# Attention backward on Trainium2: all of dS turned by the DMA crossbar in fifteen of sixteen head pairs, with a fourth dS buffer and dQ half a group later

## The chip, the core and the metric

The kernel runs on one core of one Trainium2 chip. Its engines are TensorE (PE, with its weight loads PEld), VectorE (DVE), ScalarE (ACT), GpSimd (POOL) and SyncE (SP); each works through its own instructions in order, and they meet through semaphores. SP does no arithmetic: it issues DMAs. The metric is the device time of one execution in microseconds (us). Before the change it was 2538.72 us, the median of 3 runs (2536.06 to 2540.79).

## The reference

The reference is a transformer block with adaptive layer norm, and its whole backward pass: attention with 32 heads of width 16 over 2048 tokens, a squared-ReLU MLP, and the gradients of ten inputs. The output and all gradients are returned. What matters here is attention:

```python
def _A_ref(x, wqkv, wo):
    B, S, D = x.shape            # 1, 2048, 512
    H = 32
    Dh = D // H                  # 16
    qkv = (x @ wqkv).reshape(B, S, 3, H, Dh).transpose(2, 0, 3, 1, 4)
    q, k, v = qkv[0], qkv[1], qkv[2]
    scores = jnp.einsum('bhqd,bhkd->bhqk', q, k) * Dh ** (-0.5)
    p = _softmax(scores, axis=-1)
    o = jnp.einsum('bhqk,bhkd->bhqd', p, v)
    return o.transpose(0, 2, 1, 3).reshape(B, S, D) @ wo
...
_out, _vjp = jax.vjp(_f, A_x, A_wqkv, A_wo, B_w1, B_b1, B_w2, B_b2, c, w_mod)
_grads = _vjp(grad_out)
```

For each head the backward pass computes P again from Q and K, then dP = dO V^T, dS = P (dP - rowsum), dK = dS^T Q, dV = P^T dO and dQ = dS K. The first two of the gradients sum over queries and the last over keys, so dS is wanted with queries on the partitions and, turned, with keys on the partitions.

## The kernel before, in words

The stages follow each other: forward attention, MLP forward and backward, attention backward (`attn_bwd`, L1429), and an end stage (`phase6`) with the gradients of Wqkv, of the modulation and of x. The change is in attention backward.

**Loops.** The heads are taken two at a time: 8 quads `g` of four heads, each with two pairs `jp`, so 16 pairs. In each pair `c` runs over 4 chunks of 512 keys, and `ib0` over 4 groups of G = 4 query blocks of 128. A pair thus has 16 groups, the stage 256. In a group, `i` runs over 4 units; a unit is one query block by one key chunk for both heads (`a` = 0, 1).

**One unit.** For each head PE makes the scores `st` (L1584, 64 rows of K, 512 columns) and, for the unit before (`last`), the product `dp` (L1509); ACT takes exp of `st` into `pu` (L1587); DVE multiplies `dp` by `pu` into dS (L1513). `st` and `dp` have three PSUM buffers each. In every second unit PE adds two older units to the dK and dV sums (`kv_two`, `kv`, L1455, 8 matmuls); in the others it adds up to dQ (`dq`, L1478). After the last query block of a chunk ACT copies the dK and dV sums out (`kvT`, L1458). At a pair's end these are turned on PE and copied by ACT (`turn`, L1468 and L1472, in two halves), and dQ is scaled by DVE (L1483), turned on PE (`turn_q`, L1491) and copied by ACT.

**Odd groups.** `off(c, ib)` is true in every second group. There one of the eight products of a group (unit 0, second head) goes to another place: ACT copies `dp` to SBUF (L1521) and POOL multiplies (L1522). DVE does 15 products in two groups, POOL one.

**Turning dS.** A group's dS is one buffer `ds` of 128 x 4096 bf16, 32 blocks of 128 x 128; there are three (`self.dsp`, pool `p5ds`). `turn_ds` (L1535) is called in the group's unit 2. In odd groups it only takes a destination `dsT` (four buffers). In even groups it turns the first four blocks on PE into an `st` buffer (L1543), and ACT copies them to `dsT` (L1544). When the last product of the group is made, `dS` (L1524) has SP issue one transposing DMA (L1530) for the rest: 32 blocks in odd groups, 28 in even ones.

**dQ.** When that DMA is issued, eight entries of four matmuls each go to `pendq`. In units 0 and 2 of each group, while more than 4G = 16 entries wait, four entries are taken out (eight, if more than 6G = 24 wait). A new destination or buffer waits for those who used it last; this is done by semaphores that the framework puts in.

**Order.** PE, SP and POOL follow the order of the program text; the framework orders DVE and ACT. POOL issues the loads of the next pair's operands piece by piece (`pieces`, L1573), each behind a one-element copy of dS (`tick`, L1572).

**`keep`.** A tile of 128 x 8192 bf16. Its first 2048 columns hold K of every second quad. In the last pair (g, jp) = (7, 1) the pieces that POOL issues fill all of it with the normalised x for the end stage; until then the other columns are not used.

**The end.** After the loop the remaining entries of dQ are drained in three lots, between matmuls of the end stage (`dw_mm`).

Of the kernel before, what the change touches and what calls it, by code (L numbers as in the profile page):

```python
# [9 lines left out]
BF16 = mybir.dt.bfloat16  # L10
# [9 lines left out]
P = 128  # L20
# [85 lines left out]
class K:  # L106
# [1230 lines left out]
    def phase5(self):  # L1337
        S, D, NQ, ST, DT = self.S, self.D, self.NQ, self.ST, self.DT
        nc, io = self.nc, self.io
        opa = self.open_pool("p56a", bufs=1)  # L1340
        self.pup = self.open_pool("p5pu", bufs=6)
        self.dq_t = opa.tile([P, ST, D], BF16, name="dq_t")
        self.dk_t = opa.tile([P, ST, D], BF16, name="dk_t")
        self.dv_t = opa.tile([P, ST, D], BF16, name="dv_t")
        self.opa = opa
        self.junk6 = opa.tile([P, D], F32, name="junk6")
        nc.gpsimd.memset(self.dsa_part[:], 0.0)
        assert ST * self.H == D
        self.cs = [self.csq[:], self.rl[:].rearrange("p s h -> p (s h)"), self.mod_25[:, 1, :]]
        self.parts = [self.dq_t, self.dk_t, self.dv_t]  # L1350
        self.stp = self.open_pool("p5st", bufs=3, space=PSUM)
        self.dpp = self.open_pool("p5dp", bufs=3, space=PSUM)
        self.kvp = self.open_pool("p5kv", bufs=1)
        self.dsp = self.open_pool("p5ds", bufs=3)
        self.dtp = self.open_pool("p5dt", bufs=4)
        self.accp = self.open_pool("p5acc", bufs=1, space=PSUM)
        self.attn_bwd()
# [71 lines left out]
    def attn_bwd(self):  # L1429
# [7 lines left out]
        tc, nc = self.tc, self.nc  # L1437
        S, D, H, NQ, ST, SC = self.S, self.D, self.H, self.NQ, self.ST, self.SC
        G = 4
# [7 lines left out]
        pend, pendq, turnq = [], [], []  # L1447
# [12 lines left out]
        def turn(g, jp, kvT, s0):  # L1460

            if kvT is None:
                return turn_q(g, jp)
            h0 = 4 * g + 2 * jp
            n = ST // 2
            tp = stp.tile([P, n, P], BF16, name="st")
            for st in range(n):
                nc.tensor.transpose(tp[:, st, :], kvT[:, (s0 + st) * P:(s0 + st + 1) * P], self.ident[:])  # L1468
            v = tp[:].rearrange("p s (t a e) -> p t s a e", t=2, a=2)
            for t, dst in enumerate((self.dk_t, self.dv_t)):  # L1470
                d = dst[:, s0:s0 + n, h0 * DH:(h0 + 2) * DH].rearrange("p s (a d) -> p s a d", a=2)
                nc.scalar.copy(d, v[:, t, :, :, 0:DH])  # L1472
# [31 lines left out]
        def dP(u, a):  # L1504

            (T, g, jp, c, ib, kvT, pu, dsg, i, grp) = u
            rd = slice(64 - 64 * jp, 128 - 64 * jp)
            dp = dpp.tile([P, 512], F32, name="dp")
            nc.tensor.matmul(dp[:], lhsT=T["dOT"][rd, ib * P:(ib + 1) * P],  # L1509
                             rhs=masked["VT"][a][rd, 512 * c:512 * (c + 1)], start=True, stop=True)  # L1510
            if a == 1 and i == 0 and off(c, ib):
                return dp
            nc.vector.tensor_tensor(dsg[:, i, a], dp[:], pu[:, a, :], ALU.mult)  # L1513

        def off(c, ib):
            return (c * SC + ib // G) % 2 == 1

        def dP_pool(u, dp):
            (T, g, jp, c, ib, kvT, pu, dsg, i, grp) = u
            f = (self.junk6, self.csq)[(c * SC + ib // G) // 2 % 2]  # L1520
            nc.scalar.copy(f[:], dp[:])  # L1521
            nc.gpsimd.tensor_tensor(dsg[:, i, 1], f[:], pu[:, 1, :], ALU.mult)  # L1522

        def dS(u):  # L1524

            (T, g, jp, c, ib, kvT, pu, dsg, i, grp) = u
            pend.append((T, g, jp, c, ib, kvT, pu, dsg[:, i]))
            if i == G - 1:
                dsT, n = grp
                nc.sync.dma_start_transpose(dsT[:, n:, :], dsg[:].rearrange("p i a k -> p (i a k)")[:, n * P:])  # L1530
                for a in range(2):
                    for sub in range(4):
                        pendq.append((T, g, jp, c, ib - G + 1, a, sub, dsT))

        def turn_ds(dsg, grp, skip):  # L1535

            dsT = dtp.tile([P, 8 * G, P], BF16, name="dsT")
            grp.extend((dsT, 0 if skip else 4))
            if skip:
                return  # L1540
            tp = stp.tile([P, 4, P], BF16, name="st")
            for b in range(4):
                nc.tensor.transpose(tp[:, b, :], dsg[:, 0, 0, b * P:(b + 1) * P], self.ident[:])  # L1543
            nc.scalar.copy(dsT[:, 0:4, :], tp[:])  # L1544

        tick = self.tick
        T = self.T0
        last = None
        for g in range(NQ):
            for jp in range(2):  # L1550
                if jp == 0:
                    if g + 1 < NQ:
                        Tn, later = self.load_group(g + 1)
                    else:
                        Tn, later = None, self.wq_pieces(1) + self.load_wmt()
                    cut = len(later) // 2 if Tn else len(later)
                    pieces = self.pair_pieces(g, 1) + later[:cut]
                    later = later[cut:]
                elif g + 1 < NQ:
                    pieces = self.pair_pieces(g + 1, 0) + later  # L1560
                else:
                    pieces = [(self.xhat1_6[:, st, :], self.xhat1_d.rearrange("(st p) d -> p st d", p=P)[:, st, :])
                              for st in range(ST)]
                kvT = kvp.tile([P, S], BF16, name="kvT")
                total = len(pieces)
                for c in range(SC):
                    c0 = 512 * c
                    for ib0 in range(0, ST, G):
                        m = c * (ST // G) + ib0 // G
                        while pieces and (total - len(pieces)) * SC * ST <= m * G * total:  # L1570
                            if last:
                                nc.gpsimd.tensor_copy(tick[:], last[7][0:1, 0, 0, 0:1])  # L1572
                            nc.gpsimd.dma_start(*pieces.pop(0))  # L1573
                        dsg, grp = self.dsp.tile([P, G, 2, 512], BF16, name="ds"), []
                        for i in range(G):
                            ib = ib0 + i
                            q = slice(ib * P, (ib + 1) * P)
                            if turnq and i == 2:
                                turn(*turnq.pop(0))
                            pu = self.pup.tile([P, 2, 512], BF16, name="pu")  # L1580
                            for a in range(2):
                                stt = stp.tile([P, 512], F32, name="st")
                                rs = slice(64 * jp, 64 * jp + 64)
                                nc.tensor.matmul(stt[:], lhsT=T["QT"][rs, q], rhs=masked["KT"][a][rs, c0:c0 + 512],  # L1584
                                                 start=True, stop=True)
                                held = dP(last, a) if last else None
                                nc.scalar.activation(pu[:, a, :], stt[:], ACT.Exp, scale=self.scale)  # L1587
                                if held is not None:
                                    dP_pool(last, held)
                            if last:  # L1590
                                dS(last)
                            last = (T, g, jp, c, ib, kvT, pu, dsg, i, grp)
                            if i % 2 == 1 and len(pend) >= 4:
                                kv_two()
                            elif i % 2 == 0 and len(pendq) > 4 * G:
                                for _ in range(8 if len(pendq) > 6 * G else 4):
                                    dq(pendq.pop(0))
                            if i == 2:
                                turn_ds(dsg, grp, off(c, ib))
            T = Tn  # L1600
        with tc.manual_schedule(engines=ALL):
            for t in (2, 0):
# [339 lines left out]
```

## Time and profile before

| what | value |
|---|---|
| median of 3 runs | 2538.72 us |
| the profiled execution, its own time | 2543.74 us |
| its span, first to last instruction | 2542.0 us |
| granted TensorE clock, mean | 0.995 |
| first and last transposing DMA of dS issued at | 1179.3 and 2419.8 us |
| all 40-slice shares of PE, DVE and ACT in that stretch | 0.9 or more, but for its ends |
| DVE products `ds` (L1513) | 1920, mean 680 ns, 1168.3 us busy |
| ACT exps `pu` (L1587) | 2048, mean 646 ns, 1077.5 us busy |
| ACT copies of four turned blocks (L1544) | 128, mean 596 ns, 76.3 us busy |
| PE turnings of dS (L1543) | 512, 50.8 us busy |
| transposing DMAs of dS (L1530) | 256, median 7.5 us from issue to landing |

The profile is one execution as the hardware profiler recorded it. A group of instructions has one line: line of code, engine, operation, what it writes and reads, shape and count; then its busy time, the mean of one in ns, and the idle time of the engine just before them with what ended it. The busy time of a group is a union, and the mean of one runs until its result is written, so that instructions that follow each other closely overlap: a row with 2048 exps of mean 646 ns is 1077.5 us busy. An instruction of SP's queue that issues a DMA is not counted as work, but its duration is recorded. The timeline merges instructions of one kind that follow each other without a gap, and gives the idle time before them in brackets.

### The profile page before, as it was taken

To read this page: it belongs to the slowest core of one execution; us is meant where nothing else is said; L and a number is where in the kernel's file an instruction comes from. 1 tells how busy PE (TensorE), PEld (TensorE's weight loads), DVE (VectorE), ACT (ScalarE), POOL (GpSimd) and SP (SyncE) were. 2 spreads that over 40 slices of the span, in tenths; PEclk is the share of its full clock that TensorE was granted. 3 is DMA by queue.
4 is the path that set the end of the run, shared out by engine and by line. 5 is a ranking of instruction groups with operands and counts; after the bars stand their busy time and mean duration, and the time that the engine had idled before them with its cause. 6 is when DMAs were issued, how large, how long until landed. Compare 5 with 4: busy or idle time off the path is not lost.

```text
span 2542.0 us, 76903 instructions
## 1 busy us (share of the span) xinstructions
PE 2439.2 (96%) x30791; PEld 1108.4 (44%) x30791; DVE 1694.4 (67%) x3519; ACT 2297.5 (90%) x3773; POOL 714.1 (28%) x1289
## 2 busy tenths in 40 slices
PE   8999999999999999999999999999999999999998
PEld 4555555555555554663333333333333333333343
DVE  6222223422332343677999999999999999999957
ACT  7999999999999997435999999999999999999945
POOL 2344521320131031354222222222222222222223
PEclk9999999999999999999999999999999999999999
DMA  4589652440351053799999999999999999999996
GB/s 165 133 184 210 169 106 80 103 109 30 107 134 50 22 159 105 160 190 212 224 220 216 213 218 220 223 223 217 216 216 220 220 219 217 217 226 235 231 221 181
DMA packets 1260558, 446.30 MB, mean 176 GB/s; under 512 B 1204052, under 2 KB 1228246, under 8 KB 1260198
## 3 DMA queue, kind: packets, MB, share of 16 engines
q1 hardware_dynamic: 1219654, 336.29, 70.5%
q0 software_dynamic: 38464, 104.04, 13.9%
q8 instruction: 241, 3.95, 0.7%
q10 hardware_dynamic: 2080, 1.05, 0.1%
q14 instruction: 119, 0.97, 0.1%
HBM read 75.83 MB, written 64.49 MB: 55 GB/s over the span
## 4 chain that ended last, share of the span: by engine, by line
PE 55%; ACT 26%; DMA 12%; issue 4%; DVE 2%; POOL 0%; SPq 0%; DVEq 0%; ACTq 0%; POOLq 0%
ACT pu L391 17%; PE st L1584 14%; DMA dsT<-ds 9%; PE st L388 8%; PE acckv L1455 7%; ACT pu L1587 7%; PE accq L1478 4%; PE accbank L322 3%; PE dp L1509 3%; PE dps L1050 2%; PE pps L1237 2%; PE dp L1635 2%; PE dps L995 1%; PE st L1543 1%; PE pps L631 1%
## 5 line engine op out<-in xcount | busy, mean ns | idle before, releaser
L1513 DVE TENSOR_TENSOR ds<-dp,pu 128x512 bf16<-128x512 f32 x1920 | 1168.3, 680 | 68.8 <-PE dp L1509 52.3
L1587 ACT ACTIVATE pu<-st 128x512 bf16<-128x512 f32 x2048 | 1077.5, 646 | 53.0 <-PE st L1584 21.3
L391 ACT ACTIVATE pu<-st 128x1024 bf16<-128x1024 f32 x992 | 912.3, 1077 | 4.6 <-PE st L388 4.4
L388 PE MATMUL st<-QTm,KTq 128*128 128x512 bf16 x1984 | 588.6, 377 | 19.7 <-ACT pu L391 6.0
L322 PEld LDWEIGHTS <-pu 128*128 128x128 bf16 x8192 | 347.1, 96 | 236.4 <-issue 3.5
L322 PE MATMUL accbank<-Vaug,pu 128*128 128x17 bf16 x8192 | 357.5, 171 | 1.2 <-ACT Vaug L522 0.9
L1509 PE MATMUL dp<-kvm,q 64*128 64x512 bf16 x1024 | 356.5, 383 | 1.3 <-DVE g2w L1056 0.7
L1509 PE MATMUL dp<-kvm,dOTg 64*128 64x512 bf16 x1024 | 354.9, 381 | 0.0
L1584 PE MATMUL st<-kvm,QTg 64*128 64x512 bf16 x1024 | 326.4, 380 | 17.4 <-ACT pu L1587 10.0
L1584 PE MATMUL st<-kvm,q 64*128 64x512 bf16 x1024 | 327.2, 382 | 15.7 <-ACT pu L1587 9.1
L388 PEld LDWEIGHTS <-KTq 128*128 128x128 bf16 x1984 | 188.3, 96 | 177.4 <-issue 125.5
L1522 POOL TENSOR_TENSOR ds<-junk,pu 128x512 bf16<-128x512 f32 x64 | 73.8, 1153 | 311.5 <-ACT junk L1521 311.5
L302 POOL DMA_DIRECT2D QTm<-QTq_d x124 | 63.5, 514 | 342.7 <-PE st L388 321.3
L1455 PE MATMUL acckv<-ds,q 128*16 128x512 bf16 x1024 | 154.5, 382 | 0.0
L1455 PE MATMUL acckv<-pu,q 128*16 128x512 bf16 x1024 | 154.5, 382 | 0.0
L1455 PE MATMUL acckv<-ds,Qg 128*16 128x512 bf16 x1024 | 154.4, 381 | 0.0
L1455 PE MATMUL acckv<-pu,dOg 128*16 128x512 bf16 x1024 | 154.0, 381 | 0.0
L1522 POOL TENSOR_TENSOR ds<-csq,pu 128x512 bf16<-128x512 f32 x64 | 73.8, 1153 | 277.8 <-ACT csq L1521 277.8
L329 DVE RECIPROCAL rl<-accbank 128x4 f32<-128x4 f32 x128 | 22.9, 179 | 159.1 <-PE accbank L322 158.8
L1572 POOL COPY tick<-ds 1x1 bf16<-1x1 bf16 x251 | 44.3, 176 | 297.3 <-DVE ds L1513 297.2
L1584 PEld LDWEIGHTS <-q 64*128 64x128 bf16 x1024 | 60.5, 94 | 134.5 <-issue 102.5
L1584 PEld LDWEIGHTS <-QTg 64*128 64x128 bf16 x1024 | 60.2, 94 | 132.2 <-issue 98.9
(387 smaller groups left out, 3189.0 us busy)
## 6 DMA issues: line engine op xcount, KB each, us to landing
KTq<-KTq_d POOLq DMA_DIRECT2D x24, 512.0 KB, 3.9
duT_d<-auT POOLq DMA_DIRECT2D x3, 1792.0 KB, 8.0
aT_d<-rT POOLq DMA_DIRECT2D x3, 1792.0 KB, 11.7
KTq_d<-KTq SPq DMA_DIRECT2D x32, 128.0 KB, 2.1
QTq_d<-ev_fm SPq DMA_DIRECT2D x32, 128.0 KB, 4.2
ktm_d<-ev_tm POOLq DMA_DIRECT2D x32, 128.0 KB, 2.5
VTq_d<-vT POOLq DMA_DIRECT2D x4, 1024.0 KB, 6.7
dsT<-ds SPq DMA_TRANSPOSE x256, 7.5
```

The source lines that it names most:

```text
L302: nc.gpsimd.dma_start(QTm[j][32 * j:32 * j + 32, :], self.QTq_d[g, 32 * j:32 * j + 32, 512 * qc:512 * (qc + 1)])
L322: nc.tensor.matmul(acc[:, a, sub, :], lhsT=pu[:, a, sub * P:(sub + 1) * P], rhs=Vaug[:, kb, h, :], start=(kb == 0 and a == 0 and sub == 0) ...
L388: nc.tensor.matmul(stt[:, a, :], lhsT=KT[:, kb * P:(kb + 1) * P], rhs=QTm[2 * jp + a][:], start=True, stop=True)
L391: nc.scalar.activation(pu[:], stt[:], ACT.Exp, scale=self.scale)
L1050: nc.tensor.matmul(pt[:], lhsT=a[st], rhs=g_tm[:, st, :], start=(st == 0), stop=(st == ST - 1))
L1455: nc.tensor.matmul(acckv[r:r + DH, :], lhsT=T[n][:, ib, col:col + DH], rhs=src[:, a, :], start=(ib == 0), stop=(ib == ST - 1))
L1478: nc.tensor.matmul(accq[32 * i:32 * i + 32, ib0 // G, :], lhsT=T["K"][:, 4 * c + sub, col:col + 32], rhs=dsT[:, (i * 2 + a) * 4 + sub, :], ...
L1509: nc.tensor.matmul(dp[:], lhsT=T["dOT"][rd, ib * P:(ib + 1) * P], rhs=masked["VT"][a][rd, 512 * c:512 * (c + 1)], start=True, stop=True)
L1513: nc.vector.tensor_tensor(dsg[:, i, a], dp[:], pu[:, a, :], ALU.mult)
L1522: nc.gpsimd.tensor_tensor(dsg[:, i, 1], f[:], pu[:, 1, :], ALU.mult)
L1584: nc.tensor.matmul(stt[:], lhsT=T["QT"][rs, q], rhs=masked["KT"][a][rs, c0:c0 + 512], start=True, stop=True)
L1587: nc.scalar.activation(pu[:, a, :], stt[:], ACT.Exp, scale=self.scale)
```

## The change

In all pairs but the last, `turn_ds` skips PE and ACT in even groups too, and the DMA turns all 32 blocks of every group. In the last pair it is as before. The pool of three dS buffers becomes three fixed tiles and a fourth that lies in columns 2048 to 6143 of `keep`; the last pair uses the three alone, since `keep` is then loaded for the end stage. Entries of dQ are taken out while more than 5G = 20 wait (eight, if more than 7G = 28).

```diff
@@ -1351,7 +1351,9 @@
         self.stp = self.open_pool("p5st", bufs=3, space=PSUM)
         self.dpp = self.open_pool("p5dp", bufs=3, space=PSUM)
         self.kvp = self.open_pool("p5kv", bufs=1)
-        self.dsp = self.open_pool("p5ds", bufs=3)
+        dsp = self.open_pool("p5ds", bufs=1)
+        self.ds_ring = [dsp.tile([P, 8 * 512], BF16, name=f"ds{k}")[:] for k in range(3)]
+        self.ds_ring.append(self.keep[:, ST * P:ST * P + 8 * 512])
         self.dtp = self.open_pool("p5dt", bufs=4)
         self.accp = self.open_pool("p5acc", bufs=1, space=PSUM)
         self.attn_bwd()
@@ -1527,7 +1529,7 @@
             pend.append((T, g, jp, c, ib, kvT, pu, dsg[:, i]))
             if i == G - 1:
                 dsT, n = grp
-                nc.sync.dma_start_transpose(dsT[:, n:, :], dsg[:].rearrange("p i a k -> p (i a k)")[:, n * P:])
+                nc.sync.dma_start_transpose(dsT[:, n:, :], dsg.rearrange("p i a k -> p (i a k)")[:, n * P:])
                 for a in range(2):
                     for sub in range(4):
                         pendq.append((T, g, jp, c, ib - G + 1, a, sub, dsT))
@@ -1545,7 +1547,7 @@
 
         tick = self.tick
         T = self.T0
-        last = None
+        last, n_ds = None, 0
         for g in range(NQ):
             for jp in range(2):
                 if jp == 0:
@@ -1571,7 +1573,9 @@
                             if last:
                                 nc.gpsimd.tensor_copy(tick[:], last[7][0:1, 0, 0, 0:1])
                             nc.gpsimd.dma_start(*pieces.pop(0))
-                        dsg, grp = self.dsp.tile([P, G, 2, 512], BF16, name="ds"), []
+                        ring = self.ds_ring[:3] if (g, jp) == (NQ - 1, 1) else self.ds_ring
+                        dsg, grp = ring[n_ds % len(ring)].rearrange("p (i a k) -> p i a k", i=G, a=2), []
+                        n_ds += 1
                         for i in range(G):
                             ib = ib0 + i
                             q = slice(ib * P, (ib + 1) * P)
@@ -1592,11 +1596,11 @@
                             last = (T, g, jp, c, ib, kvT, pu, dsg, i, grp)
                             if i % 2 == 1 and len(pend) >= 4:
                                 kv_two()
-                            elif i % 2 == 0 and len(pendq) > 4 * G:
-                                for _ in range(8 if len(pendq) > 6 * G else 4):
+                            elif i % 2 == 0 and len(pendq) > 5 * G:
+                                for _ in range(8 if len(pendq) > 7 * G else 4):
                                     dq(pendq.pop(0))
                             if i == 2:
-                                turn_ds(dsg, grp, off(c, ib))
+                                turn_ds(dsg, grp, (g, jp) != (NQ - 1, 1) or off(c, ib))
             T = Tn
         with tc.manual_schedule(engines=ALL):
             for t in (2, 0):
```

PE loses 480 turnings with their 480 weight loads, and ACT 120 copies; 120 transposing DMAs have 32 blocks in place of 28. Nothing is added on DVE or POOL. On PE the dQ matmuls of an entry stand one half group later; at a pair's end the scaling of dQ (L1483) stands behind the 23rd of the next pair's products on DVE, where it stood behind the 19th; the turning of dQ on PE stays where it was. After the loop 112 dQ matmuls follow, where 96 did.

## The prediction

> **What bounds the kernel now.** I read the page first, then the stage's groups, then DVE's timeline, then ACT's timeline in one double group, then the queue of the transposing DMAs.
>
> ```profile
> PE 2439.2 (96%) x30791; PEld 1108.4 (44%) x30791; DVE 1694.4 (67%) x3519; ACT 2297.5 (90%) x3773; POOL 714.1 (28%) x1289
> ...
> L1513 DVE TENSOR_TENSOR ds<-dp,pu 128x512 bf16<-128x512 f32 x1920 | 1168.3, 680 | 68.8 <-PE dp L1509 52.3
> L1587 ACT ACTIVATE pu<-st 128x512 bf16<-128x512 f32 x2048 | 1077.5, 646 | 53.0 <-PE st L1584 21.3
> ```
>
> The shares alone say that PE and ACT bind. In windows of 20 us inside the stage ACT is busy 19.6, PE 19.4 and DVE 19.0, so all three look full, and the shares settle nothing. DVE's timeline does (start, length, operation, idle time before it):
>
> ```profile
> 1503.97 9.06 DVE L1513 TENSOR_TENSOR ds<-dp,pu 128x512 bf16<-128x512 f32 x15 [0.56 <-PE dp L1509]
> 1513.48 9.12 DVE L1513 TENSOR_TENSOR ds<-dp,pu 128x512 bf16<-128x512 f32 x15 [0.45 <-PE dp L1509]
> 1522.83 9.06 DVE L1513 TENSOR_TENSOR ds<-dp,pu 128x512 bf16<-128x512 f32 x15 [0.23 <-PE dp L1509]
> 1532.34 9.12 DVE L1513 TENSOR_TENSOR ds<-dp,pu 128x512 bf16<-128x512 f32 x15 [0.45 <-PE dp L1509]
> 1541.68 9.06 DVE L1513 TENSOR_TENSOR ds<-dp,pu 128x512 bf16<-128x512 f32 x15 [0.23 <-PE dp L1509]
> ```
>
> Two groups (a double) are 15 products in one unbroken run of 9.06 us, 0.604 each, and one gap, always before the first product of the odd group's unit 1, just after the product that POOL takes. So DVE is the clock of this stage, and a change pays only as far as it closes these gaps. A double lasts 9.29 us with the short gap and 9.57 with the long one (differences of first starts). A pair has eight doubles; numbered by the pair's group 0, 2, ..., 14, undisturbed ones last 10.12, 10.49, 9.57, 9.29, 9.57, 9.29, 9.57, 9.29, together 77.2. The 14 pairs from 1257.7 to 2346.4 take 77.8 on average, so 0.6 a pair is disturbance.
>
> *Why 0.23.* Around 1636 us PE's timeline has dp for POOL at 1636.52, as soon as DVE frees its slot; then 0.54 of dK/dV matmuls from 1636.82, the next scores and dp from 1637.36, and DVE starts at 1637.89. From the freed slot to that start are some 1.4 us, in which DVE has two products, 1.2. No turning lies in that path: the change does not touch it.
>
> *Why 0.45.* These are the doubles in which ACT copies out the dK/dV sums:
>
> ```profile
> 1508.42 1.08 ACT L1587 ACTIVATE pu<-st 128x512 bf16<-128x512 f32 x2 [0.30 <-issue]
> 1509.39 0.59 ACT L1544 COPY dsT<-st 128x512 bf16<-128x512 bf16 x1
> 1509.86 1.12 ACT L1587 ACTIVATE pu<-st 128x512 bf16<-128x512 f32 x2
> 1510.83 0.73 ACT L1458 ACTIVATE kvT<-acckv,kvs 128x512 bf16<-128x512 f32 x1
> 1511.39 2.12 ACT L1587 ACTIVATE pu<-st 128x512 bf16<-128x512 f32 x4
> ```
>
> The turning's copy and the sums' copy stand two exps apart. The exp at 1511.39 ends at 1512.04, and only then does PE get the score slot that it needs at 1512.09, ahead of POOL's dp. DVE's slot was free at 1511.88, so PE is 0.2 late, and the gap is longer by that.
>
> **What is removed.** On ACT 120 copies: 596 ns each, 0.47 us from start to next start. On PE 120 times four turnings, 0.33 each on the chain of waits. By groups:
>
> - *Three doubles a pair with the sums' copy.* Without the copy the exps after it start 0.43 earlier; the sums' copy can start near 1510.4 (two exps at 0.48 from 1509.43, and its matmuls end near 1510.4), and the score slot is free near 1511.7, ahead of DVE's 1511.88. The extra goes whole: 9.57 to 9.29, 0.28 x 3 = 0.84 a pair.
> - *Three doubles without it.* The gap stays 0.23: 0.
> - *The first double of a pair (10.12 and more).* Its gap is 0.86 to 1.35. PE's turning of dK/dV there (eight matmuls, 0.57 on the chain) on top of 0.23 makes 0.80; what is above is ACT's lateness as before. I take 0.25.
> - *The second (10.49).* Its gaps are 0.19 and 0.56, the latter 0.23 and 0.33 for turning dQ. The scaling of dQ (DVE, 0.60) now stands just before that gap and may fill part of it, but dQ's turning must wait for it: +0.2 to -0.24; I take -0.10.
>
> Together 1.19 a pair, x 15 = 17.9 us.
>
> **dQ half a group later.** No PE work is added in the loop. What changes is how long a DMA may take:
>
> ```profile
> L1530 SPq DMA_TRANSPOSE dsT<-ds x256: 3457/4135/7298, 1179.3 to 2419.8; - x128
> ...
>   PE accq L1478: 15.5, 30
> ...
> DMA to landing us min/median/max: 5.8/7.5/10.1
> ```
>
> The issue holds SP's queue for 4.1 us (median; min and max on both sides), the data land 7.5 after its start, and dQ waits 30 times, 15.5 us in all, wherever landing takes about 8. Half a group, 2.3 us, lifts that to about 10.3. Doubles that contain such a wait exceed their usual length by 9.4 us in all; I take back 7. On DVE's queue the moved scaling stands ahead of 0.6 us products, which is counted above. On SP nothing is passed. After the loop 16 dQ matmuls more follow: +0.3 us (16 take 0.34 on the chain). There the 1.76 us wait of dQ for a DMA at 2423.8 stays.
>
> **Four more blocks a DMA.** This is the open price. Taken apart, odd groups' DMAs (32 blocks) hold SP's queue for 4.50 us on average (median 4.25, least 3.9), even ones (28 blocks) 4.05 (least 3.46): 0.12 a block, +0.49 each, and 0.09 to the next issue. A double needs 4.05 + 4.50 now, 9.2 afterwards. After the savings above six doubles of a pair last 9.29 and the first two 9.87 and 10.39, on average 9.5. So SP's queue goes from 88% to 97% full. The packets agree: 32 blocks are 4096 packets of 256 bytes; at the steady pace of 567 packets in 0.5 us that is 3.6, but from a transfer's first packet to its last it is 4.6 on average, since loads from POOL (64 KB a group) and instruction fetches come between. The price is bounded below by 0 (all of it beside DVE's work) and above by 120 x 0.49 = 59 us. With each double's own durations in a row, one after the other, an issue is late by 0.7 us on average and by over 2.5 in one of ten; dQ's new slack of 2.3 to 2.8 covers the rest. I take +4 us, near the lower end, since the queue keeps pace on average. The fourth buffer costs nothing: DVE now waits for a DMA issued four groups ago, and none of DVE's idle time is put down to a DMA with three. If the cover goes, it is because the queue falls behind: then dQ on PE waits, and PE's scores, ACT and DVE behind it.
>
> The Trainium skill, in "VectorE: DVE Perf Modes", section "The three transpose paths", speaks against the change: 390 ns on TensorE and 1309 ns by the crossbar for a 128x128 block, and TensorE where PSUM will do. The trace has 0.33 us on PE's chain and 0.47 on ACT for four blocks, and 0.14 us a block in a DMA of 32 (4.50 / 32), which the page's single block does not show. By the page's figures 480 blocks would give an estimate of +441 us, if nothing were hidden.
>
> **Sum.** -17.9 - 7 + 4 + 0.3 = -20.6 us. On the profiled execution (2543.74, span 2542.0) that is 2523; it is 5.0 above the median of the runs, so from 2538.72 I predict **2518 us**.
>
> **Rivals.**
>
> 1. *Forecast*, 2506 to 2526, chance 0.60. The low end has all of the 9.4, 1.6 a pair and no price: -33.
> 2. *The queue binds a little*, 0.18. An issue takes 4.75 to 4.86 us instead of 4.59 with its gap; a double is then 9.5 to 9.72, and the gain shrinks to between 20 and 0: about 2530. For it: doubles with 32-block issues near 5.0, back to back (gaps of 0.09), around 1600 us. Against: the means above.
> 3. *The queue binds outright: slower*, 0.13. With no idle stretch left between transfers (median 0.5 us now) the loads and fetches fall inside them. It decides from 4.86 us an issue (half of 9.72). At 5.05 a double is 10.1, +0.38 x 120 = +46: 2584. Against: the means already contain most of those stalls.
> 4. *ACT is the bound after all*, 0.05: 120 x 0.47 = 56 us, 2483. For it: ACT busy 98%. Against: DVE's unbroken runs; all of DVE's idle time in those 14 pairs is 59.0 us, of which 41 are gaps that the change leaves (eight of 0.23 a pair, and 0.57, 0.19 and 0.33 for the turnings at its start).
> 5. *It doesn't do what it says*, 0.04: if `keep` were one object to the framework, dQ's loads of K would wait for DVE. The built program's waits show none such. Otherwise the gaps stay for another reason: 2538.
>
> **Numbers.** A difference of 0.2% (5 us) is about what a measurement of this kernel can tell from no change. Faster: 0.60 + 0.12 of case 2 + 0.05 = 0.77. Same: 0.06 of case 2, 0.02 of case 3 and 0.04 = 0.12. Slower: 0.11. The range runs from the forecast's low end, 2506, through case 2 and the start of case 3: 2545.
>
> **What would show it.** Right: DVE's runs of 15 with 0.23 in all doubles from the third on; no ACT copy between exps; dQ waits for DMAs under 10 us in all; SP's issues 8.9 to 9.3 a double. Wrong: dQ waits of tens of us with issues above 4.86 (case 3), or gaps below 0.23 (case 4). If the 0.45 gaps stay with the copies gone, my reading of ACT's lateness failed.

## The result, and the profile after

| | before | after |
|---|---|---|
| median of the runs on one chip | 2537.39 us (4 runs) | 2578.59 us (4 runs, 2576.19 to 2586.73) |
| ratio, with its 95% interval | | 1.0169 [1.0141, 1.0197] |
| profiled execution, own time and span | 2543.74, 2542.0 us | 2586.73, 2584.9 us |
| a pair, mean of the 14 whole ones | 77.74 us | 80.79 us |
| doubles 0, 2, ..., 14 of a pair, undisturbed | 10.12, 10.49, 9.57, 9.29, 9.57, 9.29, 9.57, 9.29 | 9.85, 10.25, 9.29 six times |
| two issues of transposing DMAs, mean | 8.51 us | 9.88 us |
| issues that follow the one before within 0.15 us | 24% | 98% |

The change costs 41 us, where a gain of 20 was predicted. The 14 whole pairs give 14 x 3.05 = 42.7 of the 42.9 us by which the two spans differ, so all of it is in this stage. The rows of the issues and groups are read first; in the kernel after, the same code stands two lines further down (L1515 for L1513, L1480 for L1478), and four in the loop (L1591 for L1587).

The page of after, its busy times (compare the line that the prediction shows) and four groups (busy, mean ns | idle time before, its releaser):

```profile
PE 2413.5 (93%) x30083; PEld 1059.1 (41%) x30311; DVE 1698.4 (66%) x3519; ACT 2259.5 (87%) x3653; POOL 714.6 (28%) x1289
...
L1591 ACT ACTIVATE pu<-st 128x512 bf16<-128x512 f32 x2048 | 1067.9, 620 | 131.5 <-PE dp L1511 83.0
L1515 DVE TENSOR_TENSOR ds<-dp,pu 128x512 bf16<-128x512 f32 x1500 | 915.3, 680 | 72.3 <-PE dp L1511 65.9
...
L1480 PE MATMUL accq<-dsT,Kg 128*32 128x128 bf16 x4096 | 105.5, 224 | 45.2 <-DMA dsT<-keep 23.5
L1480 PE MATMUL accq<-dsT,keep 128*32 128x128 bf16 x4096 | 104.4, 222 | 43.4 <-DMA dsT<-ds 23.5
```

PE and ACT have 26 and 38 us less to do, as intended, and stand idle for more than that: ACT's exps waited 53.0 us in all, now 131.5. The first cause is in the last two rows: dQ on PE waits for transposing DMAs. The answer on those DMAs says how much (duration of an issue in ns, min/median/max; then who waited, us and times):

```profile
L1532 SPq DMA_TRANSPOSE dsT<-ds x196: 3611/4494/8436, 1177.2 to 2461.9; - x196
L1532 SPq DMA_TRANSPOSE dsT<-keep x60: 4887/5462/8448, 1191.8 to 2383.0; - x60
...
  PE accq L1480: 87.3, 93
...
DMA to landing us min/median/max: 6.6/8.4/11.0
```

dQ waited 15.5 us before and 87.3 after. And the 60 transfers from `keep`, the fourth buffer, hold SP's queue for 5.46 us (median), those from the three tiles 4.49; not one of the 60 takes under 4.89. That difference is in no term of the prediction.

DVE's timeline shows both halves of the story. An undisturbed stretch, then a disturbed one:

```profile
1436.42 5.46 DVE L1515 TENSOR_TENSOR ds<-dp,pu 128x512 bf16<-128x512 f32 x9
1442.11 8.46 DVE L1515 TENSOR_TENSOR ds<-dp,pu 128x512 bf16<-128x512 f32 x14 [0.23 <-PE dp L1511]
1450.49 0.68 DVE L1515 TENSOR_TENSOR keep<-dp,pu 128x512 bf16<-128x512 f32 x1
1451.40 3.68 DVE L1515 TENSOR_TENSOR keep<-dp,pu 128x512 bf16<-128x512 f32 x6 [0.23 <-PE dp L1511]
1455.00 5.46 DVE L1515 TENSOR_TENSOR ds<-dp,pu 128x512 bf16<-128x512 f32 x9
```

```profile
1355.13 6.07 DVE L1515 TENSOR_TENSOR ds<-dp,pu 128x512 bf16<-128x512 f32 x10 [0.23 <-PE dp L1511]
1363.55 2.48 DVE L1515 TENSOR_TENSOR ds<-dp,pu 128x512 bf16<-128x512 f32 x4 [2.35 <-PE dp L1511]
```

In the first, two doubles last 18.58 us with two gaps of 0.23: the 0.45 is gone, as predicted. In the second DVE stands for 2.35 us, and PE's timeline of the same microseconds names the cause, a dQ that waits for the transfer from the fourth buffer, with the next scores and dp queued behind it:

```profile
1362.69 0.41 PE L1480 MATMUL accq<-dsT,Kg 128*32 128x128 bf16 x16 [2.85 <-DMA dsT<-keep]
1363.03 0.39 PE L1588 MATMUL st<-kvm,QTg 64*128 64x512 bf16 x1
1363.03 0.39 PE L1511 MATMUL dp<-kvm,dOTg 64*128 64x512 bf16 x1
```

So the engines' part of the prediction holds in undisturbed doubles and the DMA part does not. Two things can be wrong in the latter: **the place** of the fourth buffer (its transfers are slow) and **the load** (32 blocks every time are too much for the queue wherever the buffer lies). If it is the load, the next question is what an issue's time consists of beyond its packets: instruction fetches and the loads of operands are the candidates.

The traffic of after from 1778 to 1792 us, in 40 slices of 0.35 us (first row the busy tenths of the 16 DMA engines, then what they moved). The transfer from `keep` was issued at 1778.06:

```profile
DMA  9994995099999999999995199999999999990009
GB/s 293 292 336 98 211 146 5 9 197 261 227 208 219 221 213 210 233 283 306 224 77 36 12 274 200 290 290 290 289 291 288 287 291 366 271 60 12 6 15 244
```

Three levels are to be seen: some 290 GB/s at the steady pace (256-byte packets of 18 ns); 208 to 233 between 1781.5 and 1783.9, in the transfer from `keep`, where 39% of the packets take over 20 ns, up to 59; and holes below 100. In the first and third hole a 16 KB instruction fetch of 0.88 and 0.96 us is among the packets, and the transposing packets after it take 1.1 and 1.4 us; the crossbar's stream is down to a few packets for about a microsecond. Ahead of the second hole come an 8 KB fetch of 0.50 us and a load. The middle level is not all of the place's price: 26 of the 60 transfers from `keep` have under 5% of such slow packets, nearly all of them with a fetch beside them, and hold the queue for 5.31 us or more.

### The profile page after: what moved, and what is told of

It is laid out like the page before. It is cut to its first block, busy times and chain, and to the rows that moved or that the text cites. A ratio compares the mean times of both kernels' runs of the same rounds, so it can differ in the third digit from the quotient of the medians.

```text
span 2584.9 us, 75482 instructions
## 1 busy us (share of the span) xinstructions
PE 2413.5 (93%) x30083; PEld 1059.1 (41%) x30311; DVE 1698.4 (66%) x3519; ACT 2259.5 (87%) x3653; POOL 714.6 (28%) x1289
## 3 DMA queue, kind: packets, MB, share of 16 engines
q10 hardware_dynamic: 2080, 1.05, 0.1%
## 5 line engine op out<-in xcount | busy, mean ns | idle before, releaser
L1591 ACT ACTIVATE pu<-st 128x512 bf16<-128x512 f32 x2048 | 1067.9, 620 | 131.5 <-PE dp L1511 83.0
L1515 DVE TENSOR_TENSOR ds<-dp,pu 128x512 bf16<-128x512 f32 x1500 | 915.3, 680 | 72.3 <-PE dp L1511 65.9
L388 PE MATMUL st<-QTm,KTq 128*128 128x512 bf16 x1859 | 561.7, 377 | 27.0 <-ACT pu L391 6.0
L1511 PE MATMUL dp<-kvm,dOTg 64*128 64x512 bf16 x1024 | 362.1, 386 | 0.0
L1515 DVE TENSOR_TENSOR keep<-dp,pu 128x512 bf16<-128x512 f32 x420 | 264.5, 682 | 36.7 <-PE dp L1511 35.5
L1524 POOL TENSOR_TENSOR keep<-csq,pu 128x512 bf16<-128x512 f32 x60 | 69.1, 1151 | 284.9 <-ACT csq L1523 284.9
L1480 PE MATMUL accq<-dsT,Kg 128*32 128x128 bf16 x4096 | 105.5, 224 | 45.2 <-DMA dsT<-keep 23.5
L1480 PE MATMUL accq<-dsT,keep 128*32 128x128 bf16 x4096 | 104.4, 222 | 43.4 <-DMA dsT<-ds 23.5
L1480 PEld LDWEIGHTS <-Kg 128*32 128x32 bf16 x4096 | 64.9, 96 | 164.8 <-issue 164.2
L1480 PEld LDWEIGHTS <-keep 128*32 128x32 bf16 x4096 | 65.1, 95 | 163.6 <-issue 163.1
```

The lines of the kernel that those rows point to most:

```text
L388: nc.tensor.matmul(stt[:, a, :], lhsT=KT[:, kb * P:(kb + 1) * P], rhs=QTm[2 * jp + a][:], start=True, stop=True)
L1480: nc.tensor.matmul(accq[32 * i:32 * i + 32, ib0 // G, :], lhsT=T["K"][:, 4 * c + sub, col:col + 32], rhs=dsT[:, (i * 2 + a) * 4 + sub, :], ...
```

## The experiments

Each diff is against after unless it says otherwise; each ratio is to before, run on the same chip. "Aligned" means that the kernel has e1's shift of the fourth buffer as well.

### The place of the fourth buffer

As the program lays it out, the fourth buffer begins 32 bytes short of a multiple of 4096 in each partition, that is 224 above a multiple of 256; the three tiles begin at multiples of 512.

**e1_aligned**: the buffer 16 columns (32 bytes) further on, at a multiple of 4096.

```diff
-        self.ds_ring.append(self.keep[:, ST * P:ST * P + 8 * 512])
+        self.ds_ring.append(self.keep[:, ST * P + 16:ST * P + 16 + 8 * 512])
```

> The changed kernel with its fourth dS buffer 16 columns (32 bytes) further on in keep, so that it begins at a multiple of 4096 bytes as the program places it; the other three begin at multiples of 512, the changed kernel's fourth at 32 above a multiple of 64. In the changed kernel issues that read keep last 4.89 us at least and 5.46 in the median, those that read ds 3.6 and 4.49. Theory A (the place of the source: a transposing DMA that reads from an address off by 32 bytes is slower, and the lag spreads to the next ones): issues from keep fall to the others' 4.05 at least and 4.4 to 4.6 in the middle, SP's queue has pauses again, dQ waits for DMAs under 30 us in all (87 in the changed kernel), time 2515 to 2545. Theory B (sheer load: four more blocks saturate the queue): issues from keep stay above 4.8 us, time 2570 to 2590.

2549.73 us, 1.0043 [1.0027, 1.0059]. The same rows:

```profile
L1532 SPq DMA_TRANSPOSE dsT<-ds x196: 3982/4734/8397, 1175.5 to 2429.2; - x196
L1532 SPq DMA_TRANSPOSE dsT<-keep x60: 4116/4750/6679, 1190.5 to 2350.7; - x60
...
  PE accq L1480: 50.1, 62
```

Thirty-two bytes are worth 29 us (2578.59 to 2549.73; before took 2537.39 and 2537.09 beside them). It is the transfer that they change: DVE's products into the fourth buffer of after take 682 ns on average, those into the tiles 680. Transfers from the fourth buffer are now like the others, and the traffic of this kernel around one that was issued at 1618.67 shows no stretch of the middle level (1618 to 1632 us):

```profile
GB/s 290 291 288 291 289 451 207 242 286 290 289 290 290 292 289 290 288 218 255 71 3 10 21 285 290 292 291 283 285 290 290 409 197 224 227 20 266 290 289 291
```

But the kernel is still slower than before, and dQ still waits 50 us. The place is one cause, not the whole.

**e8_off_by_64**, **e12_off_by_128**, **e11_off_by_256**: the buffer 64, 128 and 256 bytes beyond the place of e1 (`ST * P + 48`, `+ 80` and `+ 144` columns), e12 and e11 in one run each.

> The changed kernel with the fourth buffer 48 columns further on: it begins 64 bytes above a multiple of 4096. If a multiple of 64 is enough, it is the aligned variant again (issues from keep 4.1 at least, 2543 to 2553); if a packet of 256 bytes must not cross a larger boundary, issues from keep are 4.9 again and the time 2570 to 2590.

> The same with 128 bytes above a multiple of 4096. If a multiple of 128 is enough: issues from keep 4.1 at least; if a packet must not cross a multiple of 256: 4.85 at least. One look.

> The changed kernel with the fourth buffer 256 bytes above a multiple of 4096. If what counts is that a packet of 256 bytes does not cross a multiple of 256: issues from keep 4.1 at least, as aligned. If a multiple of 512 is needed: 4.85 at least. One look, for the least issue from keep.

2579.84 us (1.0149 [1.0125, 1.0172]), and 2579.11 and 2560.41 where before took 2538.96. The issues from `keep` in e8, e12 and e11:

```profile
L1532 SPq DMA_TRANSPOSE dsT<-keep x60: 4842/5424/6757, 1187.2 to 2377.8; - x60
```

```profile
L1532 SPq DMA_TRANSPOSE dsT<-keep x60: 4819/5457/6262, 1194.5 to 2379.6; - x60
```

```profile
L1532 SPq DMA_TRANSPOSE dsT<-keep x60: 4130/4738/6425, 1193.4 to 2360.7; - x60
```

64 and 128 bytes above a multiple of 256 are as slow as the 224 of after, 256 is not. So it is the distance from a multiple of 256 bytes that counts, and 256 is enough. The one run of e11 is 10 us above e1's median with the same issues. Its 14 whole pairs last 78.50 us on average and e1's 78.61, so that excess lies outside them; one run does not say more.

**e9_right_side_aligned**: the fourth buffer left at the start of `keep`'s free columns, and a pad of 224 bytes put ahead of all tiles of that side, so that they all begin at multiples of 256.

```diff
+        self.open_pool("p5pad", bufs=1, side="right").tile([P, 112], BF16, name="pad5")
         xp = self.open_pool("p5x", bufs=1, side="right")
```

> The changed kernel with its fourth buffer in the old columns of keep, but everything that is opened on the right side of the memory (keep, K, Q, dO of the quads, the masked K and V) moved down by 224 bytes, so that keep and the targets of POOL's loads begin at multiples of 256 and not at 32 above a multiple of 64. Theory A: issues from keep 4.1 at least, the time at most that of the variant with the shifted buffer alone (2545 to 2555). If the loads of POOL too are slowed by where they land, less: 2530 to 2545. If 256 is not enough: 2570 to 2590.

2546.04 us, 1.0023 [1.0009, 1.0037]; issues from `keep` have a median of 4.74 us, two issues take 9.55. It confirms the 256, by another way. That the loads' targets are aligned too brings little or nothing: the intervals of e1 and e9 overlap.

### The load, the third buffer and dQ's delay

**e2_three_buffers**: all blocks by DMA and dQ later, but three buffers throughout.

```diff
-                        ring = self.ds_ring[:3] if (g, jp) == (NQ - 1, 1) else self.ds_ring
+                        ring = self.ds_ring[:3]
```

> The changed kernel with a ring of three dS buffers throughout; keep is not used for dS. Theory A: all sources begin at multiples of 512, issues have a mean of 4.6 to 4.75 us, and DVE now and then waits for a buffer; 2520 to 2560. Theory B: the load is the same as in the changed kernel, issue means stay at 4.9 and more, 2575 to 2600.

2568.55 us, 1.0124 [1.0106, 1.0141]. dQ waits 2.1 us in all, and DVE waits instead (its waits in the 14 whole pairs: us, times, longest):

```profile
DVE ds L1515 <- PE dp L1511: 32.4, 92, 1.3
DVE ds L1515 <- DMA dsT<-ds: 30.6, 36, 2.4
```

The queue is as late as before (two issues 9.68 us), and the one who waits is now DVE, for a buffer that a transfer has not yet read. A well placed fourth buffer is worth 19 us (e1); the badly placed one was 10 us worse than none.

**e3_dq_later_alone**: before, with only the two limits of dQ raised (`> 4 * G` and `> 6 * G` to `> 5 * G` and `> 7 * G`).

> The kernel before with dQ half a group later and nothing else. By the prediction the gaps on DVE stay (9.57 and 9.29 us a double), dQ's 15.5 us of waits for DMAs in the loop go nearly to 0, and the doubles with such a wait return to their usual length: 6 to 10 us less than before. Rival: these waits lie beside work that DVE has anyway, 0 to 3 us less.

2545.48 us, 1.0029 [1.0014, 1.0043]: slower by 8, where the prediction had 7 less. dQ's waits are gone (4.5 us), but in DVE's waits of the 14 pairs a DMA now appears that before did not have:

```profile
DVE ds L1513 <- PE dp L1509: 34.9, 106, 0.8
...
DVE ds L1513 <- DMA dsT<-ds: 10.2, 18, 1.6
```

With dQ late, the buffers are the next limit. Two issues also take 8.99 us here against 8.51 with the same blocks; why, these runs do not say.

**e5_no_more_load**: aligned, four buffers, dQ later, but PE turns its four blocks in every even group as before.

```diff
-                                turn_ds(dsg, grp, (g, jp) != (NQ - 1, 1) or off(c, ib))
+                                turn_ds(dsg, grp, off(c, ib))
```

> The aligned fourth buffer and dQ later, with PE turning four blocks in all even groups as in the kernel before (28 and 32 blocks). dQ later alone cost 8 us and moved waits from PE to DVE's first product of a group. Theory (that wait was for one of three buffers): with the fourth the late products go, doubles are 9.57 and 9.29 again without disturbances, time 2526 to 2533. Rival (the later dQ itself makes the transposing DMAs longer): as dQ later alone, 2540 to 2548.

2541.30 us, 1.0003 [0.9989, 1.0017]. The fourth buffer takes e3's loss away, and still nothing is gained: dQ waits 10.7 us in 8 long waits, and the pair lasts 77.83. The 7 us of the prediction are not to be had by waiting longer.

**e6_turn_in_free_doubles** and **e10_eight_in_free_group**: aligned, the same load as before (60 blocks a double on average), but PE turns only in the doubles without the sums' copy: four blocks in each of their two groups (e6: `turn_ds(dsg, grp, ib < 2 * G)`), or eight in their even group (e10, four in unit 2 and four in unit 3).

> The aligned fourth buffer and dQ later; PE turns four blocks in both groups of the doubles without the sums' copy (groups 2, 3, 6, 7 and so on) and none in the others. The DMA turns as many blocks as in the kernel before. Theory (the queue's pace and ACT's lateness are the two terms): no double above 9.3 from the third on but for few waits, 77.0 us a pair or less, time 2508 to 2522. Rival (the second turning makes ACT late in its double): these doubles go to 9.5, 2525 to 2540.

> The aligned fourth buffer and dQ later; in groups 2, 6, 10 and 14 of a pair PE turns eight blocks (in units 2 and 3) and the DMA 24; in all others the DMA turns 32. The DMA's total is that of the kernel before. The variant with turnings in both groups of these doubles lost 0.2 us in each, by the turning in the odd group. Theory: here the turnings stand in the even group, away from DVE's gap, and the doubles stay at 9.29 to 9.35: 2520 to 2532. Rival (two copies make ACT late for the odd group): 9.5 a double again, 2535 to 2542.

2538.03 us, 0.9985 [0.9971, 0.9999], and 2538.32 us, 1.0008 [0.9991, 1.0025]. In both, the doubles with the sums' copy close to 9.29 and the others open to 9.49 (the last to 9.68, the second to 10.72 and 10.85). An undisturbed pair of e6 is 77.10, where before has 77.19: a second turning in the same double has its own price, and it takes nearly the whole gain back.

**e4_mix**: aligned, PE turns four blocks only in the even groups without the sums' copy, 62 blocks a double on average.

```diff
-                                turn_ds(dsg, grp, (g, jp) != (NQ - 1, 1) or off(c, ib))
+                                turn_ds(dsg, grp, off(c, ib) or (g, jp) != (NQ - 1, 1) and ib < 2 * G)
```

> The aligned fourth buffer and dQ later, but PE turns four blocks in the even groups whose DVE gap was 0.23 us already (groups 2, 6, 10 and 14 of a pair); only groups 0, 4, 8 and 12 give all 32 blocks to the crossbar. Half of the added load, all of the gain that the prediction saw in ACT's copies. Theory A: 2512 to 2522. Theory B (load alone, half of it): SP's queue 95% full, 2515 to 2530. If the gaps of the doubles with the sums' copy do not close here, the prediction's reading of ACT is wrong.

2535.63 us, 0.9991 [0.9977, 1.0006]. All doubles from the third on have a median of 9.29 us, so taking out half the turnings closes all of the gaps; the queue (two issues 9.41 us, 93% back to back) takes most of it back, with dQ waits of 21 us. Its one profile took 2530.3, 5 less than its median; such differences are the noise of single executions.

By load, with the buffer aligned, two issues take 8.57, 8.84 and 8.67 us at 60 blocks (e5, e6, e10), 9.41 at 62 (e4) and 9.62 at 64 (e1). The prediction had 0.49 for the step from 60 to 64; it is 0.8 to 1.05.

### What the stalls are

**e7_quarter_dq**: aligned, dQ sums over a quarter of the keys, so that PE has fewer instructions; one run.

```diff
-            for i in range(G):
+            for i in range(G if sub == 0 else 0):
```

> The aligned variant of the changed kernel with three of four dQ matmuls left out (dQ is then summed over a quarter of the keys), to have fewer instructions: PE issues some 96 fewer of 270 matmuls and weight loads a double. Theory C (instruction fetches stop the transposing packets for about 1 us each: in the aligned variant nine of ten fetches have a cluster of packets over 0.6 us beside them, while loads without a fetch nearby have one in 30 cases): fetches fall from 1.6 to 1.0 or 1.1 a double, clusters from 141 to about 95, the time in which transposing packets do not flow at full pace from 2.6 to about 2.1 us a double, issues from 4.81 to 4.5. Theory D (the loads from HBM or the transposes' own pauses): clusters and issues as in the aligned variant, 4.75 to 4.85.

**e13_no_quad_loads**: aligned, the operands of quads 2 to 7 not loaded; one run.

```diff
-        return {...}, pieces
+        return {...}, pieces if g < 2 else []
```

> The aligned variant of the changed kernel without POOL's loads of the operands of quads 2 to 7 (they are then computed with those of quads 0 and 1): about six in seven of POOL's 64 KB loads in the loop are gone, the instruction fetches stay. In the aligned variant transposing packets do not flow at full pace for 2.6 us a double. If fetches make most of that and loads only their own bytes (two loads of 64 KB a double at 291 GB/s, 0.45 us): 2.1 to 2.3 us, issues 4.55 to 4.65, clusters of slow packets as often as before (nine of ten fetches). If loads make most: under 1.6 us, issues under 4.4.

e7: 2527.31 us beside 2541.41 of before. In its stage there are 1.21 fetches a double where e1 has 1.58; stretches in which four or more transposing packets take over 0.6 us go from 141 to 110, and two issues from 9.62 to 9.35. e13: 2531.25 beside 2539.16. Two issues take 8.93, half of them back to back; of its 171 fetches 71% still have such a stretch. In e1 it is 90% of 177 fetches (every one of 16 KB, two in three of those of 8 KB), and of loads with no fetch within 3 us it is 3%. So a fetch stops the transposing stream for a while, and loads add to it. Both effects are small: against the steady pace e1 loses 2.60 us a double, e7 2.34 where about 2.1 were expected, and e13 2.37, more than either expectation, while its issues, 4.47, lie between the two. Neither kernel is a remedy, since work is missing in both; e7 also spares PE matmuls, so its time is no clean price of the fetches.

### A version that beats both

**e14_mix_right_side**: e9's pad and e4's condition. **e15_before_right_side**: before with the pad alone.

> The variant in which only groups 0, 4, 8 and 12 give all 32 blocks to the crossbar, with the right side of the memory moved to multiples of 256 (fourth buffer, K and the loads' targets) instead of the fourth buffer shifted. If aligned targets help the loads: 2525 to 2533; if not: 2533 to 2539 as with the shifted buffer.

> The kernel before with the right side of the memory moved to multiples of 256 and nothing else. Its transposing DMAs already read and write at multiples of 256, only the loads' targets change. If aligned targets help the loads, 2 to 6 us less; if not, the same time.

2531.02 us, 0.9965 [0.9951, 0.9978], and 2535.16 us, 0.9992 [0.9979, 1.0005], on one chip where before took 2539.16. The first beats both kernels, by 8 us and, over two measurements, by some 47; the pad alone can't be told from nothing. e14 is e4 with the pad in place of the shift. Their intervals, [0.9951, 0.9978] and [0.9977, 1.0006], just touch, and a pair lasts 77.40 us in e14's profile and 77.18 in e4's, so that the pad does more than the shift is not shown. DVE in e14:

```profile
1519.09 5.46 DVE L1516 TENSOR_TENSOR ds<-dp,pu 128x512 bf16<-128x512 f32 x9
1524.78 8.46 DVE L1516 TENSOR_TENSOR ds<-dp,pu 128x512 bf16<-128x512 f32 x14 [0.23 <-PE dp L1512]
1533.16 0.68 DVE L1516 TENSOR_TENSOR keep<-dp,pu 128x512 bf16<-128x512 f32 x1
1534.06 3.68 DVE L1516 TENSOR_TENSOR keep<-dp,pu 128x512 bf16<-128x512 f32 x6 [0.23 <-PE dp L1512]
1537.66 5.46 DVE L1516 TENSOR_TENSOR ds<-dp,pu 128x512 bf16<-128x512 f32 x9
```

Two doubles of 9.29 us with one gap of 0.23 each: the 0.45 is gone with half of the turnings.

## Why the prediction was wrong

The forecast was 2518, and 2579 came, outside the range and on the other side. Rival 3 describes it: the queue binds outright, dQ waits, PE's scores, ACT and DVE behind it. Even its sum holds: an issue takes 4.94 us on average and 0.10 to the next, (5.04 - 4.86) x 240 = +43. That the size came out is partly luck: the measured 5.04 contains the price of the buffer's place, of which rival 3 knows nothing. Without it (e1) an issue and its gap are 4.91.

The terms, with what was measured:

| term | predicted | measured |
|---|---|---|
| ACT's and PE's lateness | -17.9 | -20.2: undisturbed pairs 77.19 to 75.84, x 15 |
| dQ half a group later | -7 | +8 alone (e3), 0 with the fourth buffer (e5) |
| four more blocks a DMA | +4 (0 to 59) | +32.5: e1's +12.6, and the -20.2 that it eats, less the tail |
| the fourth buffer | 0 | +28.9 by its place (after less e1) |
| tail | +0.3 | not seen: 122.8 and 123.9 us from DVE's last product to the end, single profiles 120 to 129 |

The right column, with 0 for dQ and 0.3 for the tail, adds up to +41.5; +41.2 was measured. The load's 32.5 is found by difference; it was not measured by itself.

- **DVE is the clock, and which gaps close: right.** 9.87, 10.39 and 9.29 were predicted for the doubles, and 9.85, 10.25 and 9.29 are there wherever nothing waits for a DMA. e4 and e14 show that turning dS in those doubles was the cause. They take out ACT's copy, PE's turnings and the `st` buffer that these use together, so which of the three it was is not separated; for the prediction's reading speaks that PE's waits for ACT's exps go with them. In the whole pairs of before and of e4 PE waited for them (us, times, longest):

```profile
PE st L1584 <- ACT pu L1587: 17.7, 50, 0.4
```

```profile
PE st L1588 <- ACT pu L1591: 1.7, 7, 0.3
```

- **"The fourth buffer costs nothing": wrong twice.** The prediction looked at who would wait for it, and not at where it lies. Its first byte could be worked out from the layout; but by that layout no transfer of before started off a multiple of 256, so its profile has no row for the price. Measured, the place costs 28.9 us. And "none of DVE's idle time is put down to a DMA with three" was true of before only: e2 and e3 have 30.6 and 10.2 us of it.
- **"So SP's queue goes from 88% to 97% full" is the step that failed for the load.** The prediction took an issue's duration, 4.50, for what the queue needs. In before the issue is the shorter of two: a transfer of 32 blocks is 4.56 us on average from first packet to last (without the first and last sixteen, which can straggle), and ahead of it the queue rests for 0.50 (median). The prediction had the 4.6 in hand and took the pause for slack. With the queue full (e1) a transfer is 4.68, nearly the same, and the pause does not vanish: its median is 0.20. That makes 4.88, and the issues follow the data: 4.81 and 0.10 to the next. Against a break-even of 4.86 this is rival 2's and 3's border, (4.91 - 4.86) x 240 = +12 of e1's +12.6.
- **"The means already contain most of those stalls": wrong.** They lay in part in the pauses. Of 9.83 us a double in e1, some 6.3 run at the steady pace. Taken in tenths of a microsecond, 1.1 of the slower rest have an instruction fetch under way, 1.0 loads alone and 1.4 neither. But slow packets outlast the fetch: taken in unbroken stretches under nine tenths of the steady pace, those with a fetch in them make 2.2, those with loads alone 0.9 and those with neither 0.5. At the steady pace 64 blocks need 7.2; the other 2.6 are stalls, and a gain on DVE's side doesn't shorten them.
- **"I take back 7": wrong.** A later consumer does not make the queue faster. It moved the wait to DVE's buffers, and with a fourth buffer to fewer and longer waits of dQ.
- **The range**: the load's upper bound, 59, would have held its 32.5, but the range took in only the start of rival 3, and nothing for the buffer's place.

Open: the 0.5 us of stretches with neither fetch nor load; the longer issues of e3; how the place lengthens those transfers that show no middle level; why a fetch on one engine stops the transposing packets of all (the runs show that it does). That aligning the three tiles or `dsT` any differently would do more was not tried.

## What to carry to other kernels

When a queue is to be filled up, take its need from the data, first packet to last plus the pause that stays between transfers that follow each other at once, and not from the duration of the instruction that issues them; and count a gain elsewhere only up to that need. A buffer that is put into a corner of another tile has a place: look up its first byte against those of the buffers it joins before it is called free. Where a wait is moved later, ask which buffer is held longer by it.

## What the runs showed of the hardware

- A 128x4096 bf16 transposing DMA from SBUF to SBUF whose source begins 64, 128 or 224 bytes above a multiple of 256 takes at least 4.82 to 4.89 us to issue (medians 5.42 to 5.46), against 4.06 to 4.13 (4.74 to 4.75) at a multiple of 256. In some of these transfers the stream runs at 208 to 233 GB/s and not 290, with 39% of the 256-byte packets over 20 ns in the stretch shown and not 18. The Trainium skill, "DMA: Bandwidth & Descriptors", section "DMA Transpose (X-bar)", asks for 32-byte alignment in SBUF; all these places have it, so it is no measure of the speed.
- One 16 KB instruction fetch (median 0.97 us on one DMA engine in e1) brings the transposing stream from 290 GB/s to under 40 for about a microsecond (median 1.3 us; every such fetch in e1 has slow packets beside it). Of the 8 KB fetches (0.31 us) two in three do.
- The steady pace is 290 GB/s, and the mean of all traffic over the 14 whole pairs of after is 224. The same page, section "Latency and other measured facts", has 261 GB/s for a case with a non-contiguous middle dimension and about 350 to 400 for a contiguous one; beyond single slices, no stretch shown here holds the latter.
